# Attention with parts of the first block: conversion steps ahead of the squares and masks, fewer of them per unit, and another order of the parts

## The chip, the cores and the metric

The kernel runs on one core of a Trainium2 chip. The metric is the device time of one execution in microseconds; it is given as a median over executions. A profile of one execution stands beside it, with every instruction of the engines: TensorE (PE, with its weight loads PEld), VectorE (DVE), ScalarE (ACT), GpSimd (POOL), and SyncE (SP), which issues nearly all transfers.

## What is computed

Three stages follow each other on 2304 tokens of width 512: a decayed linear attention (4 batches, 8 heads, 576 positions, head size 64), a block with squared relu (512 to 2048 to 512), and a mixture of four relu blocks (512 to 1024 to 512 each), weighted by normalised probabilities.

```python
scores = scale * np.matmul(q, k.transpose(0, 1, 3, 2))
ret = scores * Dmat[None, :, :, :]          # Dmat = gamma ** (i - j) for i >= j, else 0
x = np.matmul(ret, v)                       # -> (2304, 512)
r = np.maximum(x @ w_in, 0.0)
x = (r * r) @ w_out                         # w_in 512x2048, w_out 2048x512, drawn as float64
p = domain_probs / (domain_probs.sum(-1, keepdims=True) + 1e-09)
for e in range(E):                          # E = 4
    out += p[:, e:e + 1] * (np.maximum(x @ w1[e], 0.0) @ w2[e])
```

## The kernel before

Matrix products of the two blocks run in three terms: each operand is split into a high and a low part, and hi·hi, lo·hi and hi·lo are added up in one PSUM bank. So a block of 128 x 512 outputs with a contraction of 256 takes 6 matmuls of 512 columns, one with a contraction of 512 takes 12.

**The attention stage.** It runs over 16 units, a unit being one batch and a pair of heads: units 0 to 3 are batch 0, 4 to 7 batch 1, and so on. Every unit is cut into nine chunks of 64 positions. The loop at line 393 issues for unit n, in this order: the loads of unit n+3 (line 394, on SP's queue); the inner products of unit n on TensorE (`inner`, 330), which read the masked scores `pt`; the scores of unit n+1 (281); `masked(n+1)` on VectorE (292), which writes `pt`, of which there is one buffer; the first outer products of unit n (`outer(n, False)`, 402); the state updates of unit n+1 on TensorE (306) and their copy out by ScalarE and VectorE (`states`, 318); the second outer products of unit n (`outer(n, True, done)`, 405), to which line 354 adds a wait for `masked(n+1)`; more loads (406); `finish(n)` (357), in which ScalarE copies the result to `xh` and VectorE writes the difference to `xl`; and `prepare(n+2)` (253), in which GpSimd scales half of k and multiplies q by its decay, ScalarE scales the other half of k, and, for the first four units, VectorE builds a table `qd`. In the last unit the wait is on a no-op of ScalarE instead (line 400).

**Conversion of weights.** The first block's weights are 64 bit floats. They come in pieces of 256 KB through three buffers `wraw` (`load_piece`, 72), and `from_f64` (86) turns a piece into hi and lo parts of 128 x 256. It is a generator; between its yields stand one Abs on ScalarE (101), five operations on VectorE (102, 107, 109, 111, 112; the profile gives 103 and 113 for the first and the last), and a last step with the copy of hi on ScalarE and two GpSimd operations (118 to 120). After each piece the generator issues the next piece's load. `split_w1(c)` and `split_w2(c)` go through four pieces each, and `queue_weights` puts those of chunks 0 and 1 into a list `work`. `tick(n)` issues the next n steps of that list, and `drain(g)` issues steps until generator g is through. All engines run their instructions in the order of issue, so a call of `tick` decides by its place behind what the steps stand.

**Parts.** From unit 7 on, the end of a unit also issues one part of the first block's chunk 0 (table `parts`, 372). `fill1(0, g, f, bank)` (464) makes one half of the hidden layer of token group g: 12 matmuls of 128x512 into a bank of the same two buffers in which the units' results are made, then `squares` (448): relu on ScalarE, square on VectorE, and hi and lo by ScalarE and GpSimd. `fill2(0, g, ms, bank)` (471) makes two blocks of the second layer, 12 matmuls, and ScalarE copies both out. `tick(8)` stands behind the part (line 419); up to unit 6 it is `tick(5)`.

**The main stage.** After the loop, a list of jobs goes through the rest of the first block and the mixture. Jobs 0, 1 and 2 are those whose first layer was done in attention, so the loop skips them, and `pend` holds the jobs whose second layer is still to come. `layer1` and `layer2_1` hand out two steps of `work` after each half and each block (`pace`), and each job drains what it needs. In `layer2_1` (629) one group has only two of its four blocks to do:

```python
            for m in range(KT) if (c, g) != (0, 1) else (2, 3):
```

Of the kernel before, what the change touches and what calls it, by code (L numbers as in the profile page):

```python
# [6 lines left out]
F32 = mybir.dt.float32  # L7
# [16 lines left out]
KT = DM // 128  # L24
# [8 lines left out]
def tile_kernel(ctx, tc, qT, kT, kn, vn, v4d, tables, wd, w, probs, out):  # L33
# [27 lines left out]
    def f32(ap):  # L61
        return ap.bitcast(F32)
# [10 lines left out]
    def load_piece():  # L73
        if loaded[0] == len(pieces):
            return
        c, i = pieces[loaded[0]]
        loaded[0] += 1
        if c < NW1:
            r = wrp.tile([128, BC, 2], I32, name="wraw")
            nc.sync.dma_start(out=r, in_=wd[c][:, 2 * BC * i : 2 * BC * (i + 1)].rearrange("p (n t) -> p n t", t=2))  # L80
        else:
            r = wrp.tile([128, 2 * BC], F32, name="wraw")
            nc.sync.dma_start(out=r, in_=w[(c - NW1) % NW2][:, 2 * BC * i : 2 * BC * (i + 1)])
        wraw[c, i] = r
# [100 lines left out]
    def tick(n=1):  # L185
        while work and n:
            try:
                next(work[0])
                n -= 1
            except StopIteration:  # L190
                work.pop(0)

    def drain(gen=None):

        while work and (gen is None or any(g is gen for g in work)):
            tick()
# [16 lines left out]
    def attention(a, fill1, fill2):  # L213
# [4 lines left out]
        px = a.enter_context(tc.tile_pool(name="px", bufs=2, space=PSUM))  # L218
# [12 lines left out]
        def load(n):  # L231
            if n >= NU:
                return
            b, a = units[n]
            dma = nc.scalar if n == 0 else nc.sync
            qts[n] = ap.tile([128, S], F32, name="q_t")
            kts[n] = ap.tile([128, S], F32, name="k_t")
            nc.sync.dma_start(out=qts[n], in_=qT[b, a])
            dma.dma_start(out=kts[n], in_=kT[b, a])
            if n < NP:  # L240
                nc.sync.dma_start(out=tb[:, a], in_=tables[:, a])
# [38 lines left out]
        def scores(n):  # L280

            if n >= NU:
                return
            q, k = qts.pop(n), kts.pop(n)
            qks[n] = qk = pq.tile([128, 2, 512], F32, name="qk")
            for c in woven:
                u, i = place(c)
                o = slice(C * c, C * c + C)
                for j in range(2):
                    matmul(qk[half[u], j, C * i : C * i + C], k[half[j], o], q[half[j], o], True)  # L290

        def masked(n):
            if n >= NU:
                return
            a = units[n][1]
            qk = qks.pop(n)
            pts[n] = pt = ap.tile([128, 2, 5, C], F32, name="pt", bufs=1)
            mk = tb[:, a, : 2 * C].rearrange("p (j i) -> p j i", j=2)
            v = qk[:, :, : 5 * C].rearrange("p j (c i) -> p j c i", c=5)
            done = nc.vector.tensor_tensor(  # L300
                out=pt[:, :, :4, :], in0=v[:, :, :4, :], in1=mk.unsqueeze(2).to_broadcast([128, 2, 4, C]), op=ALU.mult
            )
            nc.vector.tensor_tensor(out=pt[:C, :, 4, :], in0=v[:C, :, 4, :], in1=mk[:C], op=ALU.mult)
            return done

        def updates(n):

            if n >= NU:
                return
            kvs[n] = kv = pk.tile([128, 2, 512], F32, name="kv")  # L310
            for i in range(4):
                for u in range(2):
                    for j in range(2):
                        v = vs[n][half[u], i, j, :].unsqueeze(1).to_broadcast([C, 4 - i, D])
                        o = kv[half[j], u, D * i : 4 * D].rearrange("p (c d) -> p c d", d=D)
                        matmul(o, ks[n][half[u], i, j, :], v, i == 0)
# [13 lines left out]
        def inner(n, c):  # L330

            u, i = place(c)
            b, a = units[n]
            if c == 0:
                xos[n] = px.tile([128, 2, 512], F32, name="xo")
            for j in range(2):
                v = vs[n][half[u], i, j, :] if c < 8 else v4s[b][:, a, j, :]
                o = matmul(xos[n][half[j], u, C * i : C * i + C], v, pts[n][half[u], j, i, :], i == 0)
            return o

        def after(x, y):

            sync = mybir.DependencyInfo(mybir.DependencyClass.Sync, mybir.DependencyReason.DATA)
            tc.add_manual_dep(y.ins, x.ins.name, sync)

        def outer(n, other, done=None):

            xo, st, q = xos[n], sts[n], qs[n]
            for c in (4, 1, 5, 2, 6, 3, 7, 8):
                u, i = place(c)  # L350
                j = 1 - u if other else u
                o = matmul(xo[half[j], u, C * i : C * i + C], st[half[j], c - 1, :], q[half[j], c - 1, :], False)
                if done:
                    after(done, o)
                    done = None
# [13 lines left out]
        def bank():  # L369
            return px.tile([128, 2, 512], F32, name="xo")  # L370

        parts = {
            7: lambda: fill1(0, 0, 0, bank()[:, 0, :]), 8: lambda: fill1(0, 0, 1, bank()[:, 0, :]),
            9: lambda: fill1(0, 1, 0, bank()[:, 0, :]), 10: lambda: fill1(0, 1, 1, bank()[:, 0, :]),
            11: lambda: fill2(0, 0, (0, 1), bank()), 12: lambda: fill2(0, 0, (2, 3), bank()),
            13: lambda: fill1(0, 2, 0, bank()[:, 0, :]), 14: lambda: fill1(0, 2, 1, bank()[:, 0, :]),
            15: lambda: fill2(0, 1, (0, 1), bank()),
        }
        load(0)
        load_kv(0)  # L380
# [12 lines left out]
        for n in range(NU):  # L393
            load(n + 3)
            for c in woven:
                o = inner(n, c)
            scores(n + 1)
            done = masked(n + 1)
            if n == NU - 1:
                done = nc.scalar.nop()  # L400
                after(o, done)
            outer(n, False)
            updates(n + 1)
            states(n + 1)
            outer(n, True, done)
            load_kv(n + 3)
            finish(n)
            prepare(n + 2)
            if n in (0, 1, 2):
                load_piece()  # L410
            if n == 1:
                queue_weights()
            if n == 7:
                drain(splits[split_w1, 0])
            if n == 11:
                drain(splits[split_w2, 0])
            if n in parts:
                parts[n]()
            tick(5 if n < 7 else 8)

    with tc.manual_schedule():
        yp = ctx.enter_context(tc.tile_pool(name="yp", bufs=1))
# [6 lines left out]
        gh, gl, mags = {}, {}, {}  # L429
# [34 lines left out]
        def fill1(c, g, f, h):  # L464

            if f == 0:
                gh[c, g], gl[c, g] = hidden(g)
            products1(h, c, g, f)
            squares(h, g, gh[c, g][:, f, :], gl[c, g][:, f, :])

        def fill2(c, g, ms, o):

            for i, m in enumerate(ms):
                products2(o[:, i, :], c, gh[c, g], gl[c, g], m)
            for i, m in enumerate(ms):
                nc.scalar.copy(out=yacc[g][:, m, :], in_=o[:, i, :])  # L476
# [151 lines left out]

        def layer2_1(c, g):
            hi, lo = gh.pop((c, g)), gl.pop((c, g))  # L630
            for m in range(KT) if (c, g) != (0, 1) else (2, 3):
                o = ps.tile([128, GT], F32, name="o", tag="ps")[:, : GS[g]]
                products2(o, c, hi, lo, m)
                y = yacc[g][:, m, :]
                if c == 0:
                    nc.scalar.copy(out=y, in_=o)
                else:
                    nc.vector.tensor_tensor(out=y, in0=o, in1=y, op=ALU.add)  # L638
                tick(pace[0])
                if c == NW1 - 1 and g < 2:  # L640
                    magnitude(g, m, mags[g][m])
                if c == NW1 - 1 and g == NG - 1:
                    nc.scalar.copy(out=xh[g][:, m, :], in_=y)
                    nc.gpsimd.tensor_tensor(out=xl[g][:, m, :], in0=y, in1=f32(xh[g][:, m, :]), op=ALU.subtract)
# [49 lines left out]
        yacc += [y_tile(g) for g in range(2, NG)]  # L694
        gps[:] = [gpb, gpb, gp, gp]
        sets[0] = 0
        gh.pop((0, 0)), gl.pop((0, 0))
        nc.gpsimd.memset(cvb[0][:, :128], 2.0**-7)
        nc.scalar.copy(out=ones, in_=cvb[0][:, :128])
        nc.sync.dma_start(out=pr, in_=probs)  # L700
# [6 lines left out]
        jobs = [(c, (g,)) for c in range(NW1 - 2) for g in range(NG)]  # L707
# [12 lines left out]
        rest = place(xh_, 7, 7)[:2] + place(xl_, 7, 7)[:2]  # L720
        scaled = {NW1 + 4: 2, NW1 + 8: 3}
        sa, sb = slots(0, 1), slots(2, 3, 7)
        pend = [(1, jobs[1]), (2, jobs[2])]
        for i, job in enumerate(jobs):
            if i < 3:
                continue
            c, gs = job
            g = scaled.get(c)
# [126 lines left out]
```

## Time and profile before

| what | value |
|---|---|
| time, median of 2 runs | 1280.19 us (1280.12 to 1280.27) |
| profiled execution, its own time | 1278.26 us |
| its span, first to last instruction | 1276.5 us |
| mean granted TensorE clock | 0.985 |
| PE busy | 1223.8 us, 96% of the span |
| DVE busy | 829.7 us, 65% |
| POOL busy | 512.8 us, 40% |
| ACT busy | 449.6 us, 35% |

The span is cut into two very unequal stages: attention, up to about 145 us, and the main stage. A busy share over the whole span is a mean over both and tells little of the first, so the rows below are read by stage. Granted clock is the TensorE clock that the chip let through, as a share of full speed (1.00 is 2.4 GHz, 0.50 is 1.2 GHz). A matmul's duration includes its way through the array; matmuls overlap, so the step from one start to the next tells what one costs.

### The profile page before, as it was taken

How to read it: one execution, taken by the hardware profiler on the slowest of the kernel's cores; microseconds unless marked ns; L12 is line 12 of the kernel's file. 1: busy time of each engine (PE TensorE's matmuls, PEld its weight loads, DVE VectorE, ACT ScalarE, POOL GpSimd, SP SyncE). 2: the span in 40 equal slices, each digit the busy share in tenths (PEclk: the TensorE clock that was granted, in tenths of full speed). 3: DMA queues.
4: the chain of work that ended last, by engine and by line, in shares of the span. 5: the costliest groups of instructions: out<-in, count | busy, mean ns of one | idle time of the engine just before them, and what ended most of it. 6: DMA issues, size and time to landing. Idle time of an engine off the chain costs nothing.

```text
span 1276.5 us, 19861 instructions
## 1 busy us (share of the span) xinstructions
PE 1223.8 (96%) x7600; PEld 1028.4 (81%) x7600; DVE 829.7 (65%) x1418; ACT 449.6 (35%) x1049; POOL 512.8 (40%) x622
## 2 busy tenths in 40 slices
PE   6767799999999999999999999999999999999998
PEld 5656688888888888788888888888887888888887
DVE  4554556776777768645666677565774676767665
ACT  4433443333333334442332323322334333333330
POOL 4543344554554544453233332333143434434340
PEclk9887899999999999999999999999999999999999
DMA  8632111111111100011111111111022112111111
GB/s 291 224 107 92 44 33 42 42 42 50 42 42 42 51 17 15 27 62 47 34 34 50 42 43 34 37 47 50 18 100 82 58 43 66 37 63 50 50 42 66
DMA packets 40623, 75.15 MB, mean 59 GB/s; under 512 B 4688, under 2 KB 5200, under 8 KB 40528
## 3 DMA queue, kind: packets, MB, share of 16 engines
q1 hardware_dynamic: 40240, 73.32, 17.6%
q8 instruction: 60, 0.98, 0.3%
q10 hardware_dynamic: 288, 0.56, 0.1%
q14 instruction: 35, 0.29, 0.1%
HBM read 69.14 MB, written 4.72 MB: 58 GB/s over the span
## 4 chain that ended last, share of the span: by engine, by line
PE 85%; DVE 6%; ACT 2%; issue 1%; DMA 0%; POOL 0%; DVEq 0%; ACTq 0%
PE o L662 29%; PE h L512 23%; PE h L445 16%; PE o L459 13%; PE xo L445 1%; DVE xl L596 1%; PE xo L459 1%; DVE y L603 1%; DVE r L451 1%; DVE y L569 1%; PE xo L278 1%; ACT r L450 0%; DVE y L638 0%; DVE cv_tp L111 0%; DVE cv_m L109 0%
## 5 line engine op out<-in xcount | busy, mean ns | idle before, releaser
L662 PE MATMUL o<-w2hi,ghi 128*128 128x512 f32 x576 | 224.6, 390 | 0.1
L662 PE MATMUL o<-w2hi,glo 128*128 128x512 f32 x576 | 224.2, 389 | 0.0
L662 PE MATMUL o<-w2lo,ghi 128*128 128x512 f32 x576 | 224.1, 389 | 0.0
L670 DVE SCALAR_TENSOR_TENSOR oacc<-o,pr,oacc 128x512 f32<-128x512 f32 x270 | 195.8, 744 | 38.8 <-PE o L662 38.8
L124 POOL TENSOR_TENSOR w2lo<-wraw,w2hi 128x256 fp32r<-128x256 f32 x128 | 94.5, 766 | 208.4 <-ACT w2hi L123 208.4
L512 PE MATMUL h<-xh,w1hi 128*128 128x512 f32 x448 | 174.7, 390 | 2.4 <-ACT r L525 1.7
L512 PE MATMUL h<-xl,w1hi 128*128 128x512 f32 x448 | 174.3, 389 | 0.0
L512 PE MATMUL h<-xh,w1lo 128*128 128x512 f32 x448 | 174.3, 389 | 0.0
L124 POOL TENSOR_TENSOR glo<-r,ghi 128x512 fp32r<-128x512 f32 (+1 forms) x80 | 96.9, 1211 | 175.7 <-ACT ghi L123 166.1
L445 PE MATMUL h<-xh,w1hi 128*128 128x512 f32 (+1 forms) x424 | 144.8, 341 | 1.2 <-ACT y L476 1.2
L445 PE MATMUL h<-xl,w1hi 128*128 128x512 f32 (+1 forms) x424 | 144.7, 341 | 0.0
L445 PE MATMUL h<-xh,w1lo 128*128 128x512 f32 (+1 forms) x424 | 144.6, 341 | 0.0
L124 POOL TENSOR_TENSOR w1lo<-wraw,w1hi 128x256 fp32r<-128x256 f32 x112 | 89.2, 797 | 128.8 <-ACT w1hi L123 128.8
L662 PEld LDWEIGHTS o<-w2lo,ghi 128*128 128x128 f32 x576 | 108.1, 188 | 22.7
L662 PEld LDWEIGHTS o<-w2hi,ghi 128*128 128x128 f32 x576 | 108.2, 188 | 22.4 <-DVE oacc L670 0.5
L662 PEld LDWEIGHTS o<-w2hi,glo 128*128 128x128 f32 x576 | 108.2, 188 | 21.9
L519 DVE TENSOR_TENSOR r<-h,r 128x512 f32<-128x512 f32 x96 | 66.3, 691 | 86.8 <-PE h L512 77.5
L451 DVE TENSOR_TENSOR r<-r 128x512 f32<-128x512 f32 (+1 forms) x80 | 56.2, 703 | 94.2 <-ACT r L450 94.0
L459 PE MATMUL o<-glo,w2hi 128*128 128x512 f32 (+1 forms) x308 | 113.4, 368 | 1.0 <-POOL glo L124 1.0
L459 PE MATMUL o<-ghi,w2hi 128*128 128x512 f32 (+1 forms) x308 | 113.2, 367 | 0.0
L459 PE MATMUL o<-ghi,w2lo 128*128 128x512 f32 (+1 forms) x308 | 113.1, 367 | 0.0
L512 PEld LDWEIGHTS h<-xh,w1hi 128*128 128x128 f32 x448 | 84.1, 188 | 21.3 <-ACT r L525 2.5
(110 smaller groups left out, 2122.3 us busy)
## 6 DMA issues: line engine op xcount, KB each, us to landing
wraw<-w SPq DMA_DIRECT2D x128, 256.0 KB, 3.1
wraw<-wd SPq DMA_DIRECT2D x64, 256.0 KB, 2.7
q_t<-qT SPq DMA_DIRECT2D x16, 288.0 KB, 4.2
k_t<-kT SPq DMA_DIRECT2D x15, 288.0 KB, 4.5
v_n<-vn SPq DMA_DIRECT2D x16, 256.0 KB, 4.8
out<-oacc SPq DMA_DIRECT2D x16, 256.0 KB, 2.0
k_n<-kn SPq DMA_DIRECT2D x15, 256.0 KB, 5.0
v<-v SPq DMA_DIRECT2D x4, 128.0 KB, 5.4
```

Source lines behind the costliest of these rows:

```text
L124: nc.gpsimd.tensor_tensor(out=lo, in0=src, in1=f32(hi), op=ALU.subtract)
L278: return nc.tensor.matmul(o, w, x, start=start, stop=True, skip_group_check=True)
L445: nc.tensor.matmul(h, w, x[:, k, :], start=(n == 0), stop=(n == 3 * KT - 1))
L451: nc.vector.tensor_tensor(out=r, in0=r, in1=r, op=ALU.mult)
L459: nc.tensor.matmul(o, a[:, f, 128 * m : 128 * m + 128], x[:, f, :], start=(n == 0), stop=(n == 3 * FT - 1))
L512: nc.tensor.matmul(o, a[:, i, k, :], slot(x, j)[:, k, :], start=(first and n == 0), stop=(n == 5), skip_group_check=True,)
L519: v.tensor_tensor(out=o, in0=x, in1=y, op=ALU.add)
L569: (nc.gpsimd if k == 3 else v).tensor_tensor(out=y, in0=y, in1=s, op=ALU.mult)
L596: nc.vector.tensor_tensor(out=slot(xl_, i)[:, k, :], in0=src[:, k, :], in1=f32(hi), op=ALU.subtract)
L603: nc.vector.tensor_tensor(out=o[:, k, :], in0=x[:, k, :], in1=y[:, k, :], op=ALU.subtract)
L662: nc.tensor.matmul(o, a[:, f, 128 * m : 128 * m + 128], x[:, f, :], start=(n == 0), stop=(n == 3 * FT - 1))
L670: nc.vector.scalar_tensor_tensor(out=acc, in0=o, scalar=pr[:, tt, e : e + 1], in1=acc, op0=ALU.mult, op1=ALU.add)
```

## The change

Five things change. The table of parts has another order and one part more: parts run in units 5, 6, 8, 9, 10 and so on to 15, and both halves of group 1's second layer are among them. `tick` stands ahead of the part instead of behind it, and it hands out 8 steps in units without a part and 5 in units with one. The first three pieces are loaded together in unit 0, and the conversion is queued there. The explicit drains move from units 7 and 11 to units 5 and 10. In the main stage, group 1's second layer of chunk 0 is no longer there: `layer2_1` has no special case, and `pend` starts with job 2.

```diff
+        half_bank = lambda: px.tile([128, 2, 512], F32, name="xo")
+        one = lambda g, f: fill1(0, g, f, half_bank()[:, 0, :])
+        two = lambda g, ms: fill2(0, g, ms, half_bank())
         parts = {
-            7: lambda: fill1(0, 0, 0, bank()[:, 0, :]), 8: lambda: fill1(0, 0, 1, bank()[:, 0, :]),
-            9: lambda: fill1(0, 1, 0, bank()[:, 0, :]), 10: lambda: fill1(0, 1, 1, bank()[:, 0, :]),
-            11: lambda: fill2(0, 0, (0, 1), bank()), 12: lambda: fill2(0, 0, (2, 3), bank()),
-            13: lambda: fill1(0, 2, 0, bank()[:, 0, :]), 14: lambda: fill1(0, 2, 1, bank()[:, 0, :]),
-            15: lambda: fill2(0, 1, (0, 1), bank()),
+            5: lambda: one(0, 0), 6: lambda: one(0, 1), 8: lambda: one(1, 0), 9: lambda: one(1, 1),
+            10: lambda: two(0, (0, 1)), 11: lambda: two(0, (2, 3)), 12: lambda: one(2, 0), 13: lambda: one(2, 1),
+            14: lambda: two(1, (0, 1)), 15: lambda: two(1, (2, 3)),
         }
@@ -406,17 +407,18 @@
             load_kv(n + 3)
             finish(n)
             prepare(n + 2)
-            if n in (0, 1, 2):
-                load_piece()
-            if n == 1:
+            if n == 0:
+                for _ in range(3):
+                    load_piece()
                 queue_weights()
-            if n == 7:
+            else:
+                tick(5 if n in parts else 8)
+            if n == 5:
                 drain(splits[split_w1, 0])
-            if n == 11:
+            if n == 10:
                 drain(splits[split_w2, 0])
             if n in parts:
                 parts[n]()
-            tick(5 if n < 7 else 8)
@@ -628,7 +630,7 @@
-            for m in range(KT) if (c, g) != (0, 1) else (2, 3):
+            for m in range(KT):
@@ -694,7 +696,8 @@
-        gh.pop((0, 0)), gl.pop((0, 0))
+        for g in range(2):
+            gh.pop((0, g)), gl.pop((0, g))
@@ -720,7 +723,7 @@
-        pend = [(1, jobs[1]), (2, jobs[2])]
+        pend = [(2, jobs[2])]
```

## Rows read from the trace of the kernel before

**Rows 1.** Windows: length, busy us (instructions) per engine, PEclk, DMA share, GB/s.

```profile
8.98:24.77 15.79, 10.55 (x418) 9.88 (x411) 9.47 (x20) 6.08 (x21) 6.57 (x7) 1.00 0.99 366
24.77:40.20 15.43, 9.88 (x390) 9.02 (x392) 9.15 (x25) 7.20 (x24) 8.12 (x9) 1.00 0.68 227
40.20:50.95 10.75, 9.28 (x303) 8.75 (x295) 7.03 (x17) 5.86 (x19) 6.77 (x8) 0.84 0.59 189
50.95:145.40 94.45, 67.29 (x1133) 55.02 (x1129) 47.08 (x95) 32.37 (x90) 34.97 (x39) 0.82 0.33 104
145.40:1276.50 1131.10, 1123.31 (x5316) 942.75 (x5316) 755.36 (x1258) 395.57 (x890) 453.97 (x553) 1.00 0.14 46
```

**Rows 2.** Waits of TensorE, 0 to 146 us: total us, times, longest us.

```profile
PE xo L278 <- DVE pt L300: 24.9, 10, 3.8
PE xo L278 <- issue: 5.2, 3, 1.9
...
PE kv L278 <- issue: 4.5, 2, 2.4
PE xo L278 <- ACTq L400: 3.5, 1, 3.5
PE h L445 <- ACT y L476: 1.2, 1, 1.2
```

**Rows 3.** Timeline of TensorE: start, us, what, [idle before it and its releaser].

```profile
17.23 0.62 PE L278 MATMUL xo<-q_s,st 64*64 64x64 f32 x14
...
50.34 0.68 PE L278 MATMUL xo<-q_s,st 64*64 64x64 f32 x16 [0.48 <-DVE pt L300]
...
53.90 0.69 PE L278 MATMUL xo<-pt,v_n 64*64 64x64 f32 x32
...
60.18 0.68 PE L278 MATMUL xo<-q_s,st 64*64 64x64 f32 x16 [3.35 <-DVE pt L300]
...
84.93 1.12 PE L278 MATMUL xo<-q_s,st 64*64 64x64 f32 x16 [3.77 <-DVE pt L300]
...
89.89 0.69 PE L278 MATMUL xo<-pt,v_n 64*64 64x64 f32 x32
```

**Rows 4.** Timeline of VectorE, units 7 and 8.

```profile
51.80 0.82 DVE L367 TENSOR_TENSOR xl<-xo,xh 128x512 fp32r<-128x512 f32 x2 [0.94 <-ACT xh L365]
54.63 0.69 DVE L451 TENSOR_TENSOR r<-r 128x512 f32<-128x512 f32 x1 [2.01 <-ACT r L450]
...
59.45 0.68 DVE L300 TENSOR_TENSOR pt<-qk,tb 128x512 f32<-128x512 f32 x1
...
66.05 0.69 DVE L451 TENSOR_TENSOR r<-r 128x512 f32<-128x512 f32 x1 [3.58 <-ACT r L450]
...
67.49 1.40 DVE L111 TENSOR_SCALAR cv_tp<-cv_m 128x256 int32<-128x256 int32 x1
...
71.31 0.68 DVE L300 TENSOR_TENSOR pt<-qk,tb 128x512 f32<-128x512 f32 x1
```

**Rows 5.** Groups by line and form, VectorE, 9 to 145.4 us: busy us, mean ns | idle before.

```profile
L113 DVE SCALAR_TENSOR_TENSOR cv_b<-wraw,cv_tp 128x256 f32<-128x256 uint32 x14 | 8.0, 573 | 1.1
L109 DVE SCALAR_TENSOR_TENSOR cv_m<-wraw,cv_tp 128x256 int32<-128x256 int32 x14 | 7.8, 555 | 1.0
L111 DVE TENSOR_SCALAR cv_tp<-cv_m 128x256 int32<-128x256 int32 x14 | 7.4, 527 | 0.4
L103 DVE TENSOR_SCALAR cv_tp<-cv_tp 128x256 f32<-128x256 f32 x14 | 6.9, 493 | 14.6 <-ACT cv_tp L101 14.6
...
L107 DVE TENSOR_SCALAR cv_tp<-cv_tp 128x256 int32<-128x256 int32 x14 | 6.6, 473 | 0.4
```

**Rows 6.** Timeline of GpSimd beside the slow step of rows 4.

```profile
67.47 1.27 POOL L124 TENSOR_TENSOR glo<-r,ghi 128x512 fp32r<-128x512 f32 x1 [5.24 <-ACT ghi L123]
```

**Rows 7.** Chain that ended last, in the main stage: start, us, what.

```profile
151.15 8.16 PE o L459 x36
```

**Rows 8.** Waits of SP's DMA queue, 51 to 146 us: total us, times, longest us.

```profile
SPq L80 <- DVE cv_b L113: 82.7, 11, 10.6
```

## Prediction

> **What bounds the kernel now.** I read the windows first, then TensorE's waits, then the timelines of TensorE and VectorE around one unit. The stage after 145.40 us is TensorE's own: it is busy for 1123.31 of 1131.10 us at a granted clock of 1.00 [rows 1], so there a microsecond is won only by giving TensorE less to do. The attention stage ahead of it is not. From unit 7's first part to its end, 50.95 to 145.40, TensorE works 67.29 of 94.45 us and the granted clock is 0.82 [rows 1]. What it waits for is one thing: the second outer products wait for the mask product `pt`, 24.9 us in ten waits, up to 3.8 [rows 2].
>
> The timelines show why. Call T(n) the start of unit n's second outer products; they wait for masked(n+1). T(7) is 50.34, and twelve part matmuls follow at once and are through by 53.90 [rows 3]. VectorE does the attention difference at 51.80, then stands still for 2.01 us until the part's relu is there, squares at 54.63, and only then goes through eight conversion steps, with the next mask behind them at 59.45 [rows 4]. So part, squares, conversion and mask stand one behind the other, TensorE waits 3.35 us, and T(8) is 60.18 [rows 3]. The next unit repeats it with 3.58 us of standstill on VectorE [rows 4]. After such a wait TensorE runs at its lower level: second outer products and part together, 50.34 to 53.90, took 3.56 us; after the wait before 84.93 the same work ran to 89.89, 4.96 us [rows 3].
>
> **Counting the steps.** A piece takes seven steps: five on VectorE (lines 102 to 113), one Abs on ScalarE, one that copies hi and issues two GpSimd operations and the next piece's load. Four generators of four pieces make 112. Before: 5 each in units 1 to 6, 8 from unit 7 to 15, in all 102; 10 are left for the main stage. After: 8 in units 1 to 4, 5 in 5 and 6, 8 in 7, 5 in 8 to 15, in all 90; 22 are left. The two explicit drains find their generators finished either way (28 steps are out in unit 4, 56 in unit 9), so no part comes before its weights.
>
> **Cost of a unit, after.** Five VectorE steps cost 493+473+555+527+573 = 2.62 us a piece on average over 14 pieces [rows 5], 0.52 each. Eight steps hold 5.7 of them, 3.0 us, and one handover to Abs and back, which I take as 0.5; five steps hold 3.6, 1.9 us, and the 0.5.
> - *A unit with eight steps and no part (1 to 4, 7).* The attention difference ends 2.3 us after T (51.80+0.82-50.34), then 3.5 of steps, then 0.73 from the mask's start to TensorE (59.45 to 60.18) [rows 3, 4]: 6.5 us. TensorE's own work of the unit is shorter, so VectorE sets it. Unit 1 also builds a query table, some 0.6.
> - *A unit with a part.* TensorE's own work: 60.18 less its wait of 3.35, less 50.34, is 6.5 us [rows 3]. The conversion path: 2.3 + 2.4 + squares 0.6 + 0.73 = 6.0. The path through the part: squares start 4.3 us after T (54.63) [rows 4], then 0.6 + 0.73, 5.6. The steps now fill the standstill, TensorE is the longest, and its wait is gone: 6.5 us.
> - *Parts behind an idle stretch (5 and 8, whose predecessors have no part).* TensorE comes to them after about 3 us of idling, and the lower clock adds 4.96-3.56 = 1.4 [rows 3]: 7.9.
> - *The last two.* Unit 14: 3.56, and 1.2 for the evacuation that ScalarE does ahead of the no-op that lets unit 15 go on, 4.8; unit 15: 3.56 and the same 1.2 before the first main matmul [rows 2]: 4.8.
>
> T(1) stays at 17.2 [rows 3]; unit 0 hands out no step before or after. Sum: 17.2 + (4 x 6.5 + 0.6) + 2 x 7.9 + 6.5 + 6 x 6.5 (units 6 and 9 to 13) + 2 x 4.8 = 114.7 us for the start of the main stage, against 145.40.
>
> **What else moves.** *Two blocks of the second layer* (12 matmuls) leave the main stage: 12 x 8.16/36 = 2.7 us [rows 7]; their cost in attention is in unit 15. *The first three loads* now stand together in unit 0 on SP's queue: 512 KB sooner, in front of unit 4's loads, at the 366 GB/s of that stretch [rows 1] about 1.4 us. Unit 4's data are wanted from T(2) on, a whole unit later, so I take nothing; without that slack, 1.4 us. *The later piece loads* wait on SP for VectorE's last step, 82.7 us in 11 waits, and unit loads queue behind them [rows 8]; with the steps early in the unit that wait ends sooner, so again nothing, though unit loads have to keep up with 6.5 us instead of 11. *The 22 steps left* run in the main stage at 12 a job; they are needed at its fourth job, after 36. Nothing, because two jobs cover them; without that cover 12 more steps are 6 us. *Squares now behind the steps*: the relu waits on ScalarE behind an Abs, the square behind 2.4 us of steps, and the GpSimd low part behind both; the next reader of those is a part at least two units later.
>
> *"Issue".* TensorE waited 9.7 us in five waits for nothing that the profile shows [rows 2]; all lie before 40 us, while the DMA engines were 68 to 99% busy, and none from 40.20 to 50.95, where they moved 189 GB/s [rows 1]. I read it as the instruction stream held up by data. After the change a unit moves 1.09 MB (two tiles of 288 KB, two of 256) and five sevenths of a 256 KB piece in 6.5 us, 195 GB/s, where it was about half that. Bounds: 0 (the 189 GB/s stretch) and 2 us a unit over units 5 to 13, 18 us (the 227 GB/s stretch with its 4.5 us in 15). Nearest is the former; I take 2 us. The Trainium skill (Runtime: NRT & Kernel Launch, Instruction fetch mechanics) has the stream fetched by its own DMAs in 16 KiB blocks, at a cost "mostly hidden"; by it this term is 0 and the time 2 us less, and the trace's 9.7 us speak against taking it whole.
>
> Start of the main stage 116.7, so 28.7 us sooner, and 2.7 us less in it: 31.4. The profiled execution took 1278.26 us for a span of 1276.5; its span becomes 1245. The median stands 1.9 above the profiled time, so I put the same difference on the median: **1280.2 - 31.4 = 1249 us**.
>
> **Bounds of the sum.** Faster: no issue wait (2), no slow restart in units 5 and 8 (2.8), units 1 to 4 and 7 at 6.0, where units 1 to 6 average (50.34-17.23)/6 = 5.5 now [rows 3] (2.5): 1241 to 1242. Slower: VectorE steps at the pace they have beside a busy GpSimd. From 66.05 to 71.31 a square and eight steps took 4.65 us without the square, six steps at 0.7 each [rows 4]; that makes eight-step units 7.5, five times 1.0, and part units 6.6. With a few microseconds of issue waits: 1257. That is the likeliest case's own range.
>
> **Rivals.**
> 1. *The half clock stays* (chance 0.10). If any wait of over 2.3 us is left in the part units, each part runs as slowly as at 84.93: ten parts at 1.4, two counted already, 11 us, and the wait itself, a second or more in eight units: about 1268. For it: every such wait so far brought the lower level. Against: the wait of 0.48 before 50.34 did not [rows 3], and the paths leave TensorE under 1 us.
> 2. *Instructions or data come late* (0.11). The 2 us of issue in each of units 5 to 13: 1265; in half of them, 1256. For it: units at half the length. Against: the 189 GB/s stretch.
> 3. *Slower, steps on a locked port* (0.03). The step at 67.49 took 1.40 us while GpSimd's `glo` ran from 67.47 for 1.27 [rows 4, 6]. If steps ahead of squares and mask always meet a GpSimd operation, it is the mask that pays. From T(1) to T(14) there are 13 units; to end over 2% slower they must average 11.3 us, which takes 1.4 us a step in eight-step units and 2.0 in part units; the time would be 1306. The mean of 0.52 is far from it, and GpSimd is busy for 34.97 of 94.45 us [rows 1], 37%, though in units of 6.5 us that would be some 65%. The Trainium skill (SBUF — State Buffer, Who interferes with whom) says the pair of ports is a lock and the second to issue "fully blocks" until the first is through; the trace agrees in that row (1.40 against an average of 0.53), and it speaks against putting steps ahead of masks.
> 4. *The main stage gives it back* (0.04). TensorE waits for the 22 steps or for chunk 2 behind them: 6 us, 1255.
>
> **Numbers.** The forecast has 0.72; 2% of 1280.2 is 25.6 us, 1254.6, about what a measurement can tell. Of its 0.72, some 0.67 lies below that; the mild ends of rivals 2 and 4 add 0.03. Faster by over 2%: 0.70. Within 2%: 0.26 (0.05 of the forecast, rival 1, most of 2 and 4, and 0.01 of 3). Slower by over 2%: 0.04, rival 3 and what I don't see. Range 1241 to 1263: the forecast and the milder part of rival 2.
>
> **What would show it.** Right: main stage from about 117 us; unit starts 6.5 us apart from unit 5 on; TensorE's wait for `pt` mostly in units 1 to 4 and 7, under 12 us in all, and under 1 us where a part ran; granted clock above 0.9 from unit 9 on; VectorE's wait for the relu under 8 us; nothing new in TensorE's waits of the main stage. Wrong: T(5) later than 47 (steps dearer); units of 8 us or more with parts at half clock (rival 1); "issue" over 6 us after unit 5 (rival 2); a span that falls by less than the main stage's start moved (rival 4).

## The result and the profile after

| what | before | after |
|---|---|---|
| median | 1280.19 us | 1243.53 us (1242.99 to 1244.06) |
| profiled execution, its own time | 1278.26 us | 1242.99 us |
| its span | 1276.5 us | 1241.2 us |
| start of the main stage | 145.40 us | 112.78 us |
| length of the main stage | 1131.1 us | 1128.4 us |

The ratio is 0.9714, 95% interval 0.9672 to 0.9755. Measured again in another session with five rounds it was 0.9699 (0.9682 to 0.9717), 1241.26 us. The forecast was 1249 us in 1241 to 1263: faster as forecast, and 5.5 us more of it than the sum said. In the span, 35.3 us went: 32.6 ahead of the main stage and 2.7 in it.

TensorE's waits up to the main stage, after the change (total us, times, longest us); before, the same wait for `pt` was 24.9 us in ten [rows 2]:

```profile
PE xo L278 <- DVE pt L300: 10.4, 4, 3.1
PE xo L278 <- issue: 3.3, 2, 1.9
```

Of VectorE's waits in the same stretch, the one for the relu of a part is left at 5.0 us in two, both for a part that ran at the lower clock. From 50.95 to 145.40 it had been 19.4 in six. The first line is from the kernel before, the second from the one after:

```profile
DVE r L451 <- ACT r L450: 19.4, 6, 4.3
DVE r L453 <- ACT r L452: 5.0, 2, 3.3
```

Windows after the change: units 1 to 4, unit 5, units 9 to 13, and the main stage (length; busy us and instructions of PE, PEld, DVE, ACT, POOL; granted clock; DMA share; GB/s). They answer to [rows 1]:

```profile
17.17:41.64 24.47, 15.23 (x556) 14.46 (x548) 17.31 (x43) 11.78 (x38) 14.32 (x17) 0.92 0.74 238
41.64:50.82 9.18, 9.18 (x149) 7.42 (x150) 3.92 (x10) 3.72 (x10) 3.51 (x4) 0.65 0.87 279
71.43:103.39 31.96, 31.94 (x752) 27.29 (x745) 21.15 (x45) 18.68 (x53) 18.65 (x21) 1.00 0.49 156
112.78:1241.20 1128.42, 1120.64 (x5304) 940.39 (x5304) 759.72 (x1260) 394.49 (x890) 455.50 (x554) 1.00 0.15 46
```

In units 9 to 13 TensorE is busy for 31.94 of 31.96 us at a granted clock of 1.00: five units of 6.4 us, each with a part, where one took 10 to 13 before. VectorE's timeline of unit 6 shows what fills the old standstill of [rows 4]: difference, five steps, square, mask, without a gap of note.

```profile
52.28 0.82 DVE L367 TENSOR_TENSOR xl<-xo,xh 128x512 fp32r<-128x512 f32 x2 [0.28 <-ACT xh L365]
53.02 0.47 DVE L103 TENSOR_SCALAR cv_tp<-cv_tp 128x256 f32<-128x256 f32 x1
...
54.77 0.43 DVE L113 SCALAR_TENSOR_TENSOR cv_b<-wraw,cv_tp 128x256 f32<-128x256 uint32 x1
55.12 0.68 DVE L453 TENSOR_TENSOR r<-r 128x512 f32<-128x512 f32 x1
55.80 0.69 DVE L300 TENSOR_TENSOR pt<-qk,tb 128x512 f32<-128x512 f32 x1
```

### The profile page after: what moved, and what is told of

Same layout as the page of the kernel before. It is cut to its first block, busy times and chain, and to the rows that moved or that the text cites. A ratio compares the mean times of both kernels' runs of the same rounds, so it can differ in the third digit from the quotient of the medians.

```text
span 1241.2 us, 19864 instructions
## 1 busy us (share of the span) xinstructions
PE 1213.0 (98%) x7600; PEld 1020.6 (82%) x7600; DVE 826.9 (67%) x1418; ACT 449.0 (36%) x1049; POOL 512.5 (41%) x622
## 4 chain that ended last, share of the span: by engine, by line
PE 85%; DVE 4%; ACT 1%; issue 0%; POOL 0%; ACTq 0%; DVEq 0%
PE o L664 31%; PE h L514 24%; PE h L447 17%; PE o L461 13%; DVE xl L598 1%; DVE y L605 1%; DVE y L571 1%; DVE r L453 0%; DVE y L640 0%; ACT xh L597 0%; DVE oacc L672 0%; ACT r L452 0%; ACT w1hi L123 0%; PE sm L561 0%; ACT xl L554 0%
## 5 line engine op out<-in xcount | busy, mean ns | idle before, releaser
L453 DVE TENSOR_TENSOR r<-r 128x512 f32<-128x512 f32 (+1 forms) x80 | 58.7, 734 | 77.6 <-ACT r L452 75.7
```

The lines of the kernel that those rows point to most:

```text
L453: nc.vector.tensor_tensor(out=r, in0=r, in1=r, op=ALU.mult)
```

## The experiments

The theory (A): the place of the steps counts. Ahead of the squares they use the time in which VectorE waits for TensorE's part; behind them they lengthen the path to the next mask, for which TensorE then waits, and after such a wait it runs at its lower clock. The rival (B): fewer steps per unit and the new plan of parts bring the gain. All runs have the same main stage, 1128.1 to 1128.4 us where I read it with the tenth part and 1130.9 without, so beyond these 2.5 us every difference below lies in the start of the main stage.

**Steps back behind the part (e1).**

```diff
-            else:
-                tick(5 if n in parts else 8)
             ...
             if n in parts:
                 parts[n]()
+            if n > 0:
+                tick(5 if n in parts else 8)
```

> One edit of the changed kernel: the conversion steps stand behind the part again; their number, the parts and the loads stay as changed. Theory A (the place of the steps is what counts: ahead of the squares they fill VectorE's standstill, behind them they add to the path of the next mask): a unit with a first-layer part takes part end at T+3.6, relu 0.65, square 0.6, five steps 2.5, mask 0.73, so about 8.1 us instead of 6.3; TensorE waits some 1.8 us for pt in each of eight units, 14 us, and up to 20 if the lower clock follows some of these waits. Time 1257 to 1264. Rival B (fewer steps per unit and the other plan of parts bring the gain): 1243 to 1247, waits for pt near the 10.4 us of the changed kernel.

1258.36 us, ratio 0.9835 (0.982 to 0.985); main stage from 128.93. TensorE's wait for `pt` is 21.1 us in eleven. VectorE's timeline has the old order again: a standstill of 2.02 us ahead of the square, then five steps, one of them 1.24 us long, and the mask only at 59.41.

```profile
55.72 0.69 DVE L453 TENSOR_TENSOR r<-r 128x512 f32<-128x512 f32 x1 [2.02 <-ACT r L452]
56.33 0.29 DVE L103 TENSOR_SCALAR cv_tp<-cv_tp 128x256 f32<-128x256 f32 x1
...
57.49 1.24 DVE L111 TENSOR_SCALAR cv_tp<-cv_m 128x256 int32<-128x256 int32 x1
...
59.41 0.68 DVE L300 TENSOR_TENSOR pt<-qk,tb 128x512 f32<-128x512 f32 x1
```

A's number. But 1258 is still some 20 us under the kernel before, so the place isn't all.

**The kernel before, with that one line moved (e2).** Its eight steps, its nine parts and its loads stay.

```diff
+            tick(5 if n < 7 else 8)
             if n == 7:
                 drain(splits[split_w1, 0])
             ...
             if n in parts:
                 parts[n]()
-            tick(5 if n < 7 else 8)
```

> One edit of the kernel before: its call that hands out the steps stands ahead of the part; 8 steps per unit from unit 7 on, nine parts from unit 7, loads as before. Theory A: T(7) stays near 50.3; units 7 to 13 take the conversion path, 2.3 + 3.4 + 0.6 + 0.73 = 7.0 us, T(14) = 99.5, main stage from 109 and 2.7 us more in it than in the changed kernel: time 1243 (1240 to 1248), all of the gain from a moved line. Rival B: eight steps ahead of a mask keep TensorE waiting and at the lower clock, units of 9 us and more: 1255 to 1270.

1246.48 us, ratio 0.9745 (0.9728 to 0.9762); main stage from 113.11. TensorE waits 6.7 us for `pt`, in eight waits, the longest 1.2, and the granted clock over the whole span is 0.997. T(8) to T(12) are 57.30, 64.79, 72.44, 80.09 and 87.36: 7.5 us a unit where the expected path of eight steps gave 7.0.

```profile
64.79 0.68 PE L278 MATMUL xo<-q_s,st 64*64 64x64 f32 x16 [0.99 <-DVE pt L300]
72.44 0.68 PE L278 MATMUL xo<-q_s,st 64*64 64x64 f32 x16 [1.15 <-DVE pt L300]
80.09 0.68 PE L278 MATMUL xo<-q_s,st 64*64 64x64 f32 x16 [1.17 <-DVE pt L300]
```

One moved line brings some 32 of the 36 to 39 us.

**Eight steps in every unit, ahead (e4) and behind (e10).** e4 is the changed kernel with `tick(8)` in place of `tick(5 if n in parts else 8)`; e10 is e1 with the same replacement. With e1 and the changed kernel they make four pairs of place and number.

> The changed kernel with 8 steps in every unit from 1 on, parts or not. Theory A: part units go from TensorE's 6.3 us to the conversion path of about 6.9; nine such units, 5 us: time 1247 to 1250, TensorE's wait for pt grows by 5 us in waits of under 1 us. If conversion in part units is hidden behind TensorE whatever its number: 1243 to 1245. If eight steps set off the lower clock: 1255 and more.

> The changed kernel with 8 steps in every unit and the steps behind the part: the fourth of the four pairs of place (ahead, behind) and number (5, 8 in part units). Theory A: the path of the mask is 3.6 + 0.65 + 0.6 + steps 4.5 + 0.73 = 10.1 us in part units, and the lower clock follows each wait of 3 us, 1.4 more: units of 11 us as before the change, nine or ten of them; time 1276 to 1284, so that from 8 to 5 steps is worth some 20 us behind the part and 3.5 ahead of it. Rival B (the plan of the parts and the tenth part bring a share of their own): 1265 to 1272.

| steps in a part unit | ahead of the part | behind it |
|---|---|---|
| 5 | 1243.53 and 1241.26 us (ratio 0.9714, 0.9699) | 1258.36 us (0.9835) |
| 8 | 1247.00 us (0.9746, 0.9731 to 0.9761) | 1274.46 us (0.9952, 0.9935 to 0.9968) |

Behind the part, three steps fewer are worth 16 us; ahead of it, 3.5 to 6. Moving the steps is worth 26 to 27 us at eight steps and 15 to 17 at five. In e4 some 4 us of waits for `pt`, up to 1.2 us each, stand behind units with a part, where the changed kernel has none. The two edits take away the same wait, so their gains don't add up. e10 came out just under its expected range, 5 us faster than the kernel before; 2.7 of those are the tenth part's, shorter main stage. Its timeline is that of the kernel before, waits of up to 3.9 us for `pt` and the lower level after the long ones:

```profile
54.02 1.12 PE L278 MATMUL xo<-q_s,st 64*64 64x64 f32 x16 [3.72 <-DVE pt L300]
```

**All parts in consecutive units (e5).** The first two parts move from units 5 and 6 to 6 and 7, the first drain from 5 to 6.

> The changed kernel with its first two parts in units 6 and 7 instead of 5 and 6, so that all ten parts stand in consecutive units 6 to 15. Theory A with the cold start (a part behind a unit without one runs at the lower clock after a wait of 3 us): one such start instead of two. Unit 8 goes from 7.88 to 6.3 us, main stage from 111 instead of 112.8; time 1241.8. If the clock has nothing to do with it (the long units 5 and 8 have another cause): 1243.5.

1240.14 us, ratio 0.9692 (0.9678 to 0.9707), a time that can't be told from the changed kernel's; main stage from 110.28. The trace decides here. Unit 8 takes 6.3 us (61.57 to 67.84) instead of 7.9; the one part behind an idle stretch, now in unit 6, takes 7.88 at a granted clock of 0.78. So the cold start belongs to the wait ahead of the part, not to the unit.

**Five and six steps ahead of the parts (e6, e8).** Both are e5 with fewer steps: e6 `tick(5)` in every unit and the second drain in unit 11, e8 `tick(5 if n in parts else 6)`.

> Parts together in units 6 to 15, and 5 steps in every unit: 75 in attention, 37 left for the main stage. Theory A: units 1 to 5 go back to the 5.8 us or less of the kernel before, T(6) near 46.2 instead of 47.4, the wait before it falls from 3 to 1 us, so the first part runs at the full clock (6.3 instead of 7.9): main stage from about 107.5, time 1237 to 1238. Rival (the main stage can't take 15 more steps): TensorE waits in the main stage for chunk 1 or 2, some 5 us, and the time is 1242 or more. If the cold start has another cause than the idle stretch ahead of it, unit 6 stays at 7.9 and the time is 1239.

1250.55 us, ratio 0.9775 (0.9757 to 0.9794): a miss. The first part did run warm, 45.91 to 52.21 at 1.00, but the second layer's weights came late, in attention and not in the main stage where I had put that risk:

```profile
PE xo L461 <- ACT w2hi L118: 5.5, 2, 2.8
...
PE xo L461 <- POOL w2lo L120: 2.1, 2, 1.1
```

Units 10 and 11 wait for the hi and lo parts that are issued just ahead of them, their matmuls then run at the lower level, and the units last 13.17 and 13.42 us. The main stage took the 37 steps without loss (1128.26 us).

> Parts together in units 6 to 15, 6 steps in units 1 to 5 and 5 with a part: 80 in attention, 32 left. Theory A: between the eight-step and the five-step form of it: T(6) near 46.5, wait before it 1.5 to 2 us, first part partly at the lower clock; time 1237.5 to 1239. If the number of steps ahead of the parts is hidden behind late instructions or loads anyway: 1240, as with eight.

1236.98 us, ratio 0.9669 (0.9652 to 0.9686); main stage from 107.36. With one step more in units 1 to 5 the weights are in time, the part in unit 6 takes 6.28 us at 1.00, and TensorE waits 3.5 us for `pt` in two waits. It has the lowest median of the study, by the ratios some 4 to 6 us under the changed kernel; the ratios' intervals, 0.9652 to 0.9686 and 0.9682 to 0.9717, just overlap, so this gain is likely and not shown.

**The tenth part left to the main stage (e3).**

```diff
-            14: lambda: two(1, (0, 1)), 15: lambda: two(1, (2, 3)),
+            14: lambda: two(1, (0, 1)),
```

The main stage does these two blocks, as before; unit 15 keeps its five steps (those lines of the edit are left out here).

> The changed kernel without its tenth part: unit 15 issues none, and the two blocks are done in the main stage, as in the kernel before. Theory A (the main stage is TensorE's, attention's end is not): 2.7 us more in the main stage; attention's end loses the part's 2.75 and the 1.2 of evacuation, but the first main matmuls then wait some 1.6 us for unit 15's own difference, which the part covered. Net 0 to +1.5: time 1244 to 1245. If the part costs in unit 15 what it saves later: 1243.5. If unit 15 can't cover it at all (the part stands fully on the path, and the last wait with it): 1241.

1241.74 us, ratio 0.9707 (0.9689 to 0.9724): no difference from the changed kernel that can be told. The main stage begins at 109.72 and is 2.5 us longer. From T(14) to its start it takes 7.03 us instead of 9.39, so the part costs 2.4 us in attention and saves 2.5 behind it; the other 0.7 us of the earlier start come from units ahead of T(14). The first matmul of the main stage waits for unit 15's own difference, which the part had covered:

```profile
PE h L447 <- DVE xl L367: 1.8, 1, 1.8
```

So the 2.7 us in the main stage, which my sum counted with its cost in unit 15, net to about nothing.

**The first three pieces one per unit (e7).**

> The changed kernel, with the first three pieces loaded one per unit in units 0 to 2, as before; the conversion is still queued in unit 0. Theory A: loads are hidden either way: 1243 to 1244. If the three loads together hold up unit loads or the instruction stream: 1 to 2 us less, and less of the wait called issue before 25 us.

1242.51 us, ratio 0.9712 (0.9694 to 0.973): no difference. The wait called issue was 6.5 us in three, not less.

**Each block's copy behind its own matmuls (e9).** In `fill2` of e8's kernel the copy moves into the first loop.

> Parts together in units 6 to 15 with 6 steps in units 1 to 5, and in a second-layer part each block's copy is issued right behind its own six matmuls instead of both behind all twelve. Theory: the first copy then runs beside the second block, so the evacuation ahead of the main stage takes 0.6 instead of 1.2: time 1236.4 where the form with both copies last took 1237.0. If the copy waits for the whole bank pair anyway: 1237.0 and the same wait of 1.16 us.

1242.54 us, ratio 0.9706 (0.9691 to 0.972): a miss. The wait ahead of the main stage fell to 0.67 us as expected, but the second block of the same two-bank tile now waits for the first one's copy, which stands behind the steps on ScalarE:

```profile
PE xo L461 <- ACT y L477: 5.2, 4, 2.9
```

## Why the prediction was right, and where its terms were off

**The mechanism.** The chain of part, square, steps and mask was what held TensorE, and the steps now fill VectorE's standstill: e1 and e10 bring the wait back, e2 takes it away from the kernel before with one line. The marks named for it came: `pt` waits in four places only (before 29.33, 35.17, 41.64 and 63.55 us, which belong to units 2 to 4 and 7), none where a part ran, and 10.4 us in all; VectorE's wait for the relu 5.0 us; the clock 1.00 from unit 9 on; the same waits in the main stage as before. That the steps' place and their number replace each other was not in the prediction; it took the sum of both.

**The terms.** The start of the main stage was forecast at 116.7 us and came at 112.78:
- Units 1 to 4: 24.5 us instead of 26.6. The term that was mis-sized is the step: from 9 to 112.6 us the five VectorE steps average 0.44 us where [rows 5] had 0.52. Read unit by unit, the gain lies mostly in units 2 and 3 (5.4 and 5.8 us): the stretch from the end of the difference to the mask, forecast at 3.5 us, was 2.25 and 2.83 there, but 3.45 in units 4 and 7. Unit 1 (6.8 for 7.1) was TensorE's own, with no wait for `pt` behind it.

```profile
L109 DVE SCALAR_TENSOR_TENSOR cv_m<-wraw,cv_tp 128x256 int32<-128x256 int32 x13 | 7.1, 545 | 1.3 <-issue 0.5
L113 DVE SCALAR_TENSOR_TENSOR cv_b<-wraw,cv_tp 128x256 f32<-128x256 uint32 x12 | 5.7, 475 | 1.0
L107 DVE TENSOR_SCALAR cv_tp<-cv_tp 128x256 int32<-128x256 int32 x13 | 5.6, 434 | 0.4
L103 DVE TENSOR_SCALAR cv_tp<-cv_tp 128x256 f32<-128x256 f32 x13 | 5.0, 383 | 4.5 <-ACT cv_tp L101 4.5
L111 DVE TENSOR_SCALAR cv_tp<-cv_m 128x256 int32<-128x256 int32 x13 | 4.6, 354 | 0.4
```

- Unit 5: 9.18 instead of 7.9, because the whole part ran at the lower level. This term is no fixed size: the same program gave 6.30 in another execution (last section). Unit 8 came as forecast, 7.88; unit 7 too, 6.46 for 6.5.
- Units 6 and 9 to 13: 6.27 and five of 6.39, together 38.2 instead of 39.0.
- The last two: 9.4 instead of 9.6.
- Issue: no such wait after 20 us, where I had taken 2. The lower bound of that term was right; the 2 us were a choice between two bounds.

These are 2.1 + 0.8 + 0.2 + 2.0 less 1.3, 3.8 of the 3.9 us. The length of the main stage, 2.7 us less, was exact. Of the rest of the median's 5.5 us, 1.4 are not in the span, as after the change median and profiled time stand 0.5 apart and not 1.9, and 0.2 are rounding. So the time lies near the lower end of the range, where the sum without its issue term and with shorter eight-step units stood; the third condition of that end, no slow restart, did not come.

**The rivals.** Of the parts, only those of units 5 and 8 met the half clock (1); unit 5 was over the 8 us named as this rival's sign, but as a restart behind a unit without a part. Late instructions cost nothing beyond the forecast here (2): the last such wait, 1.86 us before 19.82, lies in unit 1. The experiments had 2.9 to 8.7 us of it in their profiles, nearly all before 50 us; two executions of the changed kernel had 3.3 and 3.9, so whether the edits or the executions make that spread isn't shown. For locked ports (3) the trace shows the opposite of the fear on the whole. The slow step of 1.40 us stood beside the squares' `glo`, and ahead of the squares a step does not meet it: L111, the step of that row, fell from 527 to 354 ns on average. But a step can now meet GpSimd's product `q_s`, as in unit 1 of the changed kernel:

```profile
20.29 1.43 POOL L273 TENSOR_TENSOR q_s<-q_t,qd 128x512 f32<-128x512 f32 x1 [2.85 <-DVE cv_tp L103]
20.62 1.38 DVE L109 SCALAR_TENSOR_TENSOR cv_m<-wraw,cv_tp 128x256 int32<-128x256 int32 x1
```

By the Trainium skill (SBUF — State Buffer, Who interferes with whom), where a VectorE and a GpSimd instruction need the port pair that they share, the second to issue is blocked until the first is through; both traces agree with that rule (1.40 us beside `glo` before, 1.38 beside `q_s` after). On balance the rule spoke for the change, as the shorter steps show. That the steps moved away from `glo` is read from the timelines; that this alone made them shorter was not tested by itself. It can't be the main cause, though: in e2, with eight steps as before, VectorE's steps beside the parts take 22.0 us (46 steps, 50.5 to 107 us) instead of 26.2 (45, 50.5 to 139), while its wait for the relu falls from 19.4 us to 1.4. The main stage gave nothing back (4): 1128.26 us even with 37 steps left.

## What to carry to other kernels

Where side work is woven into a pipeline whose engines run in order, first look for an engine that stands still for another one's long piece, and issue the side work ahead of that wait, not behind it: here eight steps a unit cost some 26 us behind the wait that they did not cost ahead of it. Then compare the number of steps with what still fits beside the longest engine, and see that what the steps produce is there a unit before it is read. Two edits that take away the same wait should be tried in all four pairs; their gains are not to be added.

## What the runs showed of the hardware

In these runs the lower TensorE level costs a unit with a part 1.4 to 2.9 us, and whether it comes goes with the wait ahead of the part. Over the thirteen profiles, all 23 parts behind a wait for `pt` or the no-op of 2.34 us or more ran partly or wholly at the lower level, and none behind such a wait of 1.76 us or less did; of the six behind 2.02 to 2.24 us, two did (one each in e1 and e10) and four did not. Parts that waited for weights or a copy in their own middle (e6, e9) are left aside. How long the level lasts, the wait alone doesn't tell. In the profiled execution of the changed kernel T(5) followed a wait of 3.07 us, and unit 5 took 9.18 us at 0.65; in e7 it followed one of 3.06, and the unit took 7.69 at 0.80. The changed kernel ran once more beside others:

> The changed kernel once more, beside the others of this call: 1243.5, within 1.5; TensorE's wait for pt 10 us in four waits, parts in units 5 and 8 at the lower clock.

It took 1241.26 us (1239.43 to 1243.70), a little less than expected. In its profiled execution the same program had a wait of 1.76 us there, and the unit took 6.30 at 1.00:

```profile
41.36 0.68 PE L278 MATMUL xo<-q_s,st 64*64 64x64 f32 x16 [1.76 <-DVE pt L300]
47.66 0.68 PE L278 MATMUL xo<-q_s,st 64*64 64x64 f32 x16
```

The main stage began at 109.40 instead of 112.78, and 2.9 of these 3.4 us lie in this unit. The trace shows why the wait was shorter: here the lower level had come already in unit 4, which has no part. TensorE took 3.61 us from 34.65 to 38.26, at 0.53, for what it did in 2.10 us from 35.17 to 37.27 at 1.00, and so had less time left to wait. So a kernel near such a wait can have two times by one and the same code, and a difference of 2 or 3 us between two of its edits needs more than one execution.
